# Retention and a channel-mix block on one core: block 0's k tiles made in two steps of six products, and all steps put in a new order

## The chip, the cores and the metric

One core of one Trainium2 chip runs the whole program. The metric is device time in microseconds of one execution. Three runs of the kernel before gave 395.34, 395.37 and 395.74 us, so its median is 395.37 us.

## The reference

`q`, `k`, `v` have 4 batches, 8 heads, 768 tokens and 64 channels, in float32. The first half is retention with a decay per head, `lam`, in steps of 64 tokens; the second is a channel mix over all 512 channels, whose three products are most of the arithmetic.

```python
for b in range(nb):
    intra = np.einsum('bhic,bhjc->bhij', qb, kb) * Dmask[None]
    intra = np.einsum('bhij,bhjd->bhid', intra, vb)
    inter = np.einsum('bhid,bhde->bhie', qb * lam_pow[None], kv_state)
    out[:, :, sl] = intra + inter
    kv_state = lam_block[None, :, None, None] * kv_state + np.einsum('bhsd,bhse->bhde', kb_dec, vb)
...
xk = mu_k * x + (1.0 - mu_k) * x_prev
xr = mu_r * x + (1.0 - mu_r) * x_prev
k = np.maximum(xk @ w_k, 0.0)
v = k * k @ w_v
r = 1.0 / (1.0 + np.exp(-(xr @ w_r)))
return r * v
```

## The kernel before, in words

The tokens are cut into six blocks of 128 (n = 0 to 5), and the heads into four pairs (hp = 0 to 3). Each block goes through retention (scores, decay, values, state), the mix with the token before, and the three products with `w_r`, `w_k` and `w_v`. The weights arrive as 64-bit floats and are put together in the kernel, in block 0's time. For precision each operand of the large products is split in two float32r parts, high and low, and one product is three matmuls of 512 columns (`product`, L420): high by high, high by low, low by high. Only the first half of `w_r` is used unsplit, as float32, in block 0.

The order is written out by hand. `ORDER` (L495) is a string of steps; each step is a letter, a block (or r, k, v for a weight) and an index, and calls one function (table at L464). Every engine keeps the order in which its instructions are issued (`InOrder`, L25), and so does the queue of SyncE, SP, on which all loads are issued. The letters that matter here:

- L, N, H: loads of q, k, v tiles (512 KB, for block 0 also halves). S: load of a weight part (`stage_part`, L176; Sv0 to Sv3 are 1 MB each). c: ScalarE (ACT) copies the part's top bits into `top`. C: VectorE (DVE) puts the word together in place. D: ACT makes the high part (`hir`, `hik`, `hiv`), DVE the low part (`lor`, `lok`, `lov`).
- A scores (`sc`), a their decay (`mw`, `mv`), U state sums (`u`), u and w the next state, B, g and G values (`xp`; g is a one-element copy into `junk` that stands between B and G), q and k decays of queries and keys.
- e, E, f, F: the mix with the token before, for `xk` (small letters) and `xr` (capitals); y, x: its split in `xh` and `xl`.
- R, Q: products with `w_r` for batches 0, 1 and 2, 3 (`r_part`, L402); s: sigmoid into `rt`.
- K: products with `w_k` for one of eight column tiles f (`k_part`, L414), 12 matmuls; h: relu and square into `kf`, in block 0 both on ACT; p: split of two tiles f into `k` (k2).
- V: products with `w_v`, half of the tiles f for one batch (`v_part`, L438); o: multiply with `rt` and store.

PSUM has four buffers of one tag, "m" (`ps_m`, L74), for the tiles rp, kp, vp and from block 1 on xp. A tile that starts must wait until a buffer has been read out: a kp tile by the relu of its h, a vp tile by its o, an rp tile by its s. DMAs on SP use eight semaphores in turn, so a load also waits for the landing of the load eight places earlier.

Of the kernel before, what the change touches and what calls it, by code (L numbers as in the profile page):

```python
# [7 lines left out]
F32 = mybir.dt.float32  # L8
F32R = mybir.dt.float32r
I32 = mybir.dt.int32  # L10
U32 = mybir.dt.uint32
# [7 lines left out]
HP = H // 2  # L19
# [17 lines left out]
def tile_retention_moe(  # L37
# [36 lines left out]
    ps_m = ctx.enter_context(tc.tile_pool(name="ps_m", bufs=4, space=bass.MemoryType.PSUM))  # L74
# [9 lines left out]
    VS, Q, KT, KN = {}, {}, {}, {}  # L84
# [85 lines left out]
    def single(kind, i):  # L170
        return kind + "01"[i % 2] in SINGLE
# [202 lines left out]
    def mix(n, which, hp):  # L374
        t = ts[n, which, hp]
        o = t[:, :, 0:128]
        if n == 0 and which * HP + hp in X32:
            o = X32[which * HP + hp].rearrange("p (b i) -> p b i", b=B)
        vector.scalar_tensor_tensor(o, xp_of(n, hp), mus[:, which, hp:hp + 1], t[:, :, 0:128],
                                    op0=ALU.mult, op1=ALU.add)  # L380

    def split_x(n, which, hp):
        i = which * HP + hp
        if i not in Xhi:
            Xhi[i] = const.tile([128, 512], F32R, tag=f"x{i}", name=f"xh{i}")
        split(Xhi[i].rearrange("p (b i) -> p b i", b=B), Xlo[i].rearrange("p (b i) -> p b i", b=B), ts.pop((n, which, hp))[:, :, 0:128])
# [3 lines left out]
    def product(p, stationary, moving, first, last):  # L390

        passes = PASSES[:2 * len(moving) - 1]
        for i, (s, m) in enumerate(passes):
            tensor.matmul(p, stationary[s], moving[m], start=first and i == 0, stop=last and i == len(passes) - 1)

    def w_of(n, kind, i, c, cols):
        tiles = [W32[kind, i]] if n == 0 and single(kind, i) else [Whi[kind, i], Wlo[kind, i]]
        return [t[:, c, cols] for t in tiles]

    def x_of(n, i, cols=slice(0, 512)):  # L400
        return [t[:, cols] for t in ([X32[i]] if n == 0 and i in X32 else [Xhi[i], Xlo[i]])]

    rps, rt, kps, kfs, k2, vps = {}, {}, {}, {}, {}, {}

    def r_part(n, hp, half):
        for b in (2 * half, 2 * half + 1):
            if hp == 0:
                rps[n, b] = ps_m.tile([128, 512], F32, tag="m", name="rp")
            product(rps[n, b], x_of(n, HP + hp, slice(b * 128, b * 128 + 128)),
                    w_of(n, "r", hp // 2, hp % 2, slice(0, 512)), hp == 0, hp == HP - 1)  # L410

    def r_out(n, b):
        rt[n, b] = work.tile([128, 512], F32, tag="rt", name="rt", bufs=4)
        scalar.activation(rt[n, b], rps.pop((n, b)), AF.Sigmoid)  # L414

    def k_part(n, f):
        kps[n, f] = p = ps_m.tile([128, 512], F32, tag="m", name="kp")
        for hp in range(HP):
            product(p, w_of(n, "k", hp // 2 + f // 4 * 2, hp % 2, slice(f % 4 * 128, f % 4 * 128 + 128)), x_of(n, hp),
                    hp == 0, hp == HP - 1)  # L420

# [38 lines left out]
    def v_out(n, b):  # L460
# [6 lines left out]
        e=lambda n, hp: mix_prev(n, 0, hp), E=lambda n, hp: mix_prev(n, 1, hp),  # L467
        f=lambda n, hp: mix(n, 0, hp), F=lambda n, hp: mix(n, 1, hp),
        y=lambda n, hp: split_x(n, 0, hp), x=lambda n, hp: split_x(n, 1, hp),
        R=lambda n, hp: r_part(n, hp, 0), Q=lambda n, hp: r_part(n, hp, 1), s=r_out, K=k_part, h=k_square, p=k_split, V=v_part, o=v_out,  # L470
        S=stage_part, c=conv_top, C=conv_bits, D=conv_split)
    for step in ORDER.split():
        if step[0] == "Z":
# [19 lines left out]


ORDER = """  # L495
L01 M00 L00 Z10 d01 N01 A01 a01 H01 d02 H00 L02 k01 d00 A00 H02 U01 a00 N00 B01 L03 d03 A02 k00 u01 E01 l00 a02 H03
U00 k02 l02 u00 N02 B00 k03 N03 Sr0 A03 e00 E00 F01 U02 a03 Sr1 Sr2 U03 Sr3 Sk1 u02 u03 cr0 Sk0 e01 B03 E03 cr1 F00
B02 Cr0 f00 L11 Cr1 f01 cr2 L10 E02 R00 Cr2 F03 cr3 Q00 Q01 F02 y00 Dr2 N10 R01 Cr3 x02 e02 Q02 l01 N11 R02 x03 y01
Sk3 Dr3 Q03 N12 R03 f02 ck1 A10 ck0 e03 Ck0 L12 k11 k10 Ck1 f03 y02 Dk0 Dk1 U10 A11 U11 s00 y03 a10 s01 ck3 s02 Sk2
a11 q11 K03 h03 k12 u11 u10 q10 K01 h01 B10 g10 ck2 Sv1 Ck3 Sv0 Ck2 Dk3 A12 G10 s03 Dk2 N13 L13 cv1 K00 Sv3 a12 cv0  # L500
h00 w11 K02 h02 K07 Cv1 K06 l03 E10 Cv0 w10 e10 e11 Sv2 F10 U12 Dv0 E11 f11 f10 k13 p00 F11 p01 h07 A13 U13 q12 q13
K05 K04 cv3 Dv1 cv2 h05 Cv3 L21 a13 V00 Cv2 u13 h06 Dv3 N21 N23 h04 u12 Dv2 V02 B12 g12 A21 p02 y10 p03 G12 V01 x11
o00 x10 L20 e13 V03 y11 V04 e12 q21 N20 E12 o01 F12 f13 f12 a21 V06 V05 Dr0 o02 w12 y12 w13 L23 y13 V07 k20 A20 U20
K10 u20 E13 F13 K11 x12 a20 L22 k21 h10 K16 o03 Q10 x13 Q11 q20 h11 h16 Q12 Q13 U21 B20 A23 u21 N22 g20 A22 G20 p10
s12 k23 s13 N31 K17 h17 E21 K12 N30 q23 F21 e20 e21 a22 h12 p13 K14 f21 L30 k30 w21 K15 w20 E20 f20 h15 a23 h14 K13
k22 h13 F20 R10 x20 U23 L31 U22 B22 R11 u23 R12 g22 y21 u22 p11 q22 R13 G22 w22 o53 w23 A31 y20 A30 k31 q30 U30 E23
U31 s11 e23 e22 N33 s10 V10 a30 x21 E22 F23 L33 f22 F22 y22 f23 a31 V16 V14 p12 V17 u31 x23 V11 o10 V12 V15 x22 y23
u30 V13 o11 o12 N32 K27 o13 K26 Q20 Q21 h27 Q22 h26 Q23 p23 s22 q31 L32 B30 g30 A32 A33 G30 e31 s23 E30 f31 K24 K25
E31 e30 L41 F31 h24 K20 h20 N41 a33 q33 f30 w31 K23 w30 K21 h25 L40 F30 q32 K22 p22 h21 k32 R20 R21 k33 a32 h22 U33
k40 x30 h23 U32 y31 B32 N40 u32 R22 p20 R23 w32 y30 g32 u33 p21 G32 w33 A40 s20 A41 a41 k41 E32 U41 q41 F32 e33 e32  # L510
f33 x32 U40 q40 f32 V20 V21 u40 V22 a40 N43 N42 L42 o20 E33 s21 k42 y33 V23 B40 u41 y32 F33 g40 A42 w41 L43 x31 x33
A43 G40 o21 E41 E40 N50 Q30 e40 Q31 N51 a43 e41 F41 F40 f40 L50 Q32 Q33 s33 q42 K32 f41 V24 V25 s32 k43 K31 h32 V26
a42 K33 V27 h31 h33 K30 w40 L51 h30 K37 o22 k50 p31 R30 R31 q43 R32 R33 x40 o23 U42 h37 s31 U43 u42 u43 B42 g42 A50
A51 G42 s30 L52 q51 K34 K35 p30 h34 K36 a50 h35 E42 y41 y40 e42 a51 L53 h36 F42 e43 V32 V34 f42 f43 q50 x42 w42 p33
V30 p32 V31 y42 x41 y43 V35 o30 V33 E43 N52 o31 N53 V36 k52 V37 F43 K41 K42 o32 k51 w43 U50 x43 o33 u51 B50 g50 u50
A52 h41 A53 G50 h42 E51 a52 K43 e50 F51 h43 e51 K40 a53 E50 f50 K47 p41 F50 f51 K44 K45 h40 p40 h47 K46 h45 h46 R40
q52 R41 h44 k53 p42 R42 R43 B52 U52 u53 g52 s41 q53 s40 Q40 Q41 u52 Q42 Q43 G52 y51 s42 e53 y50 f53 s43 x50 e52 f52
p43 V42 V40 V41 x51 E52 E53 F53 o40 F52 y53 x52 y52 V43 K52 K53 V44 h53 K51 V45 o41 K54 o42 h52 V46 x53 h54 V47 p51
o43 K50 h51 Q50 K55 Q51 h50 h55 Q52 Q53 R50 s53 p50 K57 R51 s52 R52 h57 K56 h56 V52 R53 V50 p52 p53 V51 s50 V56 o50
s51 V53 V54 V55 o51 o52 V57  # L520
"""


# [60 lines left out]
```

## Time and profile before

| what | value |
|---|---|
| median of three runs | 395.37 us |
| the profiled execution: span from first to last instruction | 393.7 us |
| what lies around the span (median less span) | 1.7 us |
| TensorE matmul (PE) busy | 386.9 us, 98% of the span |
| VectorE (DVE) busy | 208.8 us, 53% |
| ScalarE (ACT) busy | 168.5 us, 43% |
| GpSimd (POOL) busy | 23.5 us, 6% |
| granted TensorE clock, mean | 1.000 |

No time of the profiled execution is given besides its span. The busy shares are means over the whole program; the rows further down go by stretch. In a timeline row the first number is the start in us from the span's start, the second how long the row lasts; "xN" merges N instructions, and a bracket says how long the engine had been idle and who ended that. A matmul of 512 columns is shown with some 0.39 us, but the next one starts 0.227 us after it.

### The profile page before, as it was taken

What the parts mean: (1) busy time and instruction counts of PE and PEld (TensorE: products, weight loads), DVE (VectorE), ACT (ScalarE), POOL (GpSimd) and SP (SyncE); (2) the same over time, 40 slices, a digit from 0 to 9 for tenths busy, and PEclk for the clock granted to TensorE, in tenths of its full rate; (3) what the DMA queues carried; (4) which work ended last, traced back from release to release, by engine and by line L of the source; (5) the groups of instructions that cost most, each with busy time, mean ns of one, the idle gap of its engine ahead of it and who ended that gap; (6) DMA issues with size and microseconds to landing.
All of it is one profiled execution on the core that took longest, in us unless ns stands there. A gap on an engine that the chain in (4) does not pass through costs nothing.

```text
span 393.7 us, 9414 instructions
## 1 busy us (share of the span) xinstructions
PE 386.9 (98%) x4154; PEld 317.5 (81%) x4154; DVE 208.8 (53%) x322; ACT 168.5 (43%) x276; POOL 23.5 (6%) x97
## 2 busy tenths in 40 slices
PE   7999999999999999999999999999999999999996
PEld 3757888888888888888888888888888888888885
DVE  4898989763377723358754026573373272232311
ACT  2798999443365412418353023542243360222300
POOL 2121010200001100100110000100000000000000
PEclk9999999999999999999999999999999999999999
DMA  7999861810320502230525001501000000000011
GB/s 265 412 407 412 305 246 55 303 45 28 116 102 11 208 27 82 81 136 2 200 68 219 0 27 42 203 19 64 28 2 1 3 27 27 28 27 0 2 42 65
DMA packets 15560, 42.64 MB, mean 108 GB/s; under 512 B 1440, under 2 KB 1824, under 8 KB 15520
## 3 DMA queue, kind: packets, MB, share of 16 engines
q1 hardware_dynamic: 11920, 35.76, 24.6%
q10 hardware_dynamic: 3600, 6.29, 4.4%
q8 instruction: 32, 0.52, 0.5%
q14 instruction: 8, 0.07, 0.1%
HBM read 35.76 MB, written 6.29 MB: 107 GB/s over the span
## 4 chain that ended last, share of the span: by engine, by line
PE 84%; ACT 8%; DMA 4%; DVE 1%; issue 1%; SPq 1%; POOL 0%; ACTq 0%; POOLq 0%
PE vp L33 32%; PE kp L33 29%; PE rp L33 14%; PE xp L33 4%; DMA wst<-w_r 2%; ACT kf L33 2%; ACT top L33 2%; PE u L33 2%; PE sc L33 2%; DMA in<-first 2%; ACT hiv L33 1%; ACT hik L33 1%; ACT ts L33 1%; SPq L33 1%; ACT xh L33 1%
## 5 line engine op out<-in xcount | busy, mean ns | idle before, releaser
L33 PE MATMUL vp<-hiv,k 128*128 128x512 f32 (+1 forms) x400 | 121.8, 382 | 0.0
L33 PEld LDWEIGHTS vp<-hiv,k 128*128 128x128 f32 x400 | 74.1, 188 | 14.6
L33 PE MATMUL vp<-lov,k 128*128 128x512 f32 (+1 forms) x200 | 76.1, 381 | 0.0
L33 PE MATMUL kp<-xh,hik 128*128 128x512 f32 x192 | 75.6, 394 | 0.3 <-ACT rt L33 0.3
L33 PE MATMUL kp<-xl,hik 128*128 128x512 f32 x192 | 74.8, 390 | 0.0
L33 PE MATMUL kp<-xh,lok 128*128 128x512 f32 x192 | 74.8, 390 | 0.0
L33 ACT ACTIVATE kf<-kp 128x512 f32<-128x512 f32 x48 | 28.3, 595 | 99.3 <-PE kp L33 84.1
L33 DVE TENSOR_TENSOR kf<-kp,kf 128x512 f32<-128x512 f32 x40 | 27.5, 690 | 67.7 <-ACT kf L33 67.6
L33 ACT ACTIVATE ts<-xp,omu 128x512 f32<-128x512 f32 x48 | 31.3, 687 | 29.8 <-DVE rt L33 12.1
L33 PEld LDWEIGHTS vp<-lov,k 128*128 128x128 f32 x200 | 37.6, 188 | 7.1
L33 PEld LDWEIGHTS kp<-xh,hik 128*128 128x128 f32 x192 | 36.0, 188 | 8.5 <-ACT rt L33 0.5
L33 PEld LDWEIGHTS kp<-xh,lok 128*128 128x128 f32 x192 | 36.0, 188 | 7.6
L33 PEld LDWEIGHTS kp<-xl,hik 128*128 128x128 f32 x192 | 36.0, 188 | 7.2
L33 DVE TENSOR_TENSOR xl<-ts,xh 128x512 fp32r<-128x512 f32 x46 | 30.9, 687 | 19.3 <-ACT xh L33 19.3
L33 DVE TENSOR_TENSOR rt<-vp,rt 128x512 f32<-128x512 f32 (+1 forms) x25 | 16.4, 666 | 45.4 <-PE vp L33 43.6
L33 ACT CAST xh<-ts 128x512 fp32r<-128x512 f32 x46 | 27.3, 617 | 25.2 <-DVE rt L33 20.3
L33 DVE SCALAR_TENSOR_TENSOR ts<-xp,mus,ts 128x512 f32<-128x512 f32 x46 | 33.4, 746 | 8.5 <-ACT ts L33 5.5
L33 DVE TENSOR_TENSOR k<-kf,k 128x1024 fp32r<-128x1024 f32 x24 | 29.2, 1222 | 13.0 <-ACT k L33 12.8
L33 PE MATMUL rp<-hir,xh 128*128 128x512 f32 x88 | 35.1, 399 | 0.0
L33 PE MATMUL rp<-hir,xl 128*128 128x512 f32 x88 | 34.3, 390 | 0.0
L33 PE MATMUL rp<-lor,xh 128*128 128x512 f32 x88 | 34.3, 389 | 0.0
L33 ACT CAST k<-kf 128x1024 fp32r<-128x1024 f32 x24 | 24.8, 1048 | 9.4 <-DVE kf L33 7.5
(58 smaller groups left out, 354.3 us busy)
## 6 DMA issues: line engine op xcount, KB each, us to landing
in<-kk SPq DMA_DIRECT2D x20, 512.0 KB, 6.4
in<-qv SPq DMA_DIRECT2D x20, 512.0 KB, 5.5
out<-rt ACTq DMA_DIRECT2D x23, 256.0 KB, 2.0
wst<-w_k SPq DMA_DIRECT2D x4, 1023.8 KB, 12.8
wst<-w_v SPq DMA_DIRECT2D x4, 1023.8 KB, 9.5
in<-first SPq DMA_DIRECT2D x4, 512.0 KB, 5.9
in<-first SPq DMA_DIRECT2D x8, 256.0 KB, 6.6
wst<-w_r SPq DMA_DIRECT2D x4, 511.8 KB, 8.8
```

Of the source, the lines that this page charges most:

```text
L33: return lambda *args, **kw: self.tc.keep_in_program_order(op(*args, **kw))
```

## The change

Two functions are reshaped and the order string is replaced as a whole. `k_part` can now be made in two steps: J (`k_begin`) opens the PSUM tile and makes the six matmuls of head pairs 0 and 1, and the later K makes the six of pairs 2 and 3; where no J came before, K makes all twelve. In the new order each of the eight k tiles of block 0 has a J; the other blocks have none. `r_part` now opens its tile with whichever pair comes first and closes it with the fourth made, so that the order of pairs is free. The work is the same: the same matmuls, casts, loads and stores.

```diff
     def r_part(n, hp, half):
         for b in (2 * half, 2 * half + 1):
-            if hp == 0:
+            first = (n, b) not in rps
+            if first:
                 rps[n, b] = ps_m.tile([128, 512], F32, tag="m", name="rp")
+            done[n, b] = done.get((n, b), 0) + 1
             product(rps[n, b], x_of(n, HP + hp, slice(b * 128, b * 128 + 128)),
-                    w_of(n, "r", hp // 2, hp % 2, slice(0, 512)), hp == 0, hp == HP - 1)
+                    w_of(n, "r", hp // 2, hp % 2, slice(0, 512)), first, done[n, b] == HP)
...
+    def k_begin(n, f):
+        k_pairs(n, f, range(HP // 2))
+
     def k_part(n, f):
-        kps[n, f] = p = ps_m.tile([128, 512], F32, tag="m", name="kp")
-        for hp in range(HP):
+        k_pairs(n, f, range(HP // 2 if (n, f) in kps else 0, HP))
+
+    def k_pairs(n, f, pairs):
+        if (n, f) not in kps:
+            kps[n, f] = ps_m.tile([128, 512], F32, tag="m", name="kp")
+        p = kps[n, f]
+        for hp in pairs:
             product(p, w_of(n, "k", hp // 2 + f // 4 * 2, hp % 2, slice(f % 4 * 128, f % 4 * 128 + 128)), x_of(n, hp),
                     hp == 0, hp == HP - 1)
...
-K05 K04 cv3 Dv1 cv2 h05 Cv3 L21 a13 V00 Cv2 u13 h06 Dv3 N21 N23 h04 u12 Dv2 V02 B12 g12 A21 p02 y10 p03 G12 V01 x11
...
+p00 Sv2 p01 cv2 u12 J07 K07 cv3 h04 h07 u13 Cv2 K06 V00 k21 a13 h05 h06 B12 A21 Cv3 g12 Dv2 p02 p03 G12 Dv3 N22 V02 w13
```

How the new string moves instructions is shown at three places. The first is ACT in block 0, between the split of k2's second tile and the first relus of the second half of k. Before (p01, h07, cv3, Dv1, cv2, h05):

```order
L33 CAST k_1_778<-kf 128x2x512 [waits DVE_49]
L33 ACTIVATE kf<-kp 128x512 [waits DVE_49,PE_49]
L33 ACTIVATE kf<-kf 128x512 [waits Activation_49]
L33 CAST top_101<-wst 128x1024 [waits DMAHW7_49]
L33 CAST hiv_845<-wst 128x1024
L33 CAST top_100<-wst 128x1024 [waits DMAHW0_49]
L33 ACTIVATE kf<-kp 128x512 [waits DVE_49,PE_49]
```

With the change (p01, cv2, cv3, h04, h07):

```order
L33 CAST k_1_826<-kf 128x2x512 [waits DVE_49]
L33 CAST top_100<-wst 128x1024 [waits DMAHW2_49]
L33 CAST top_101<-wst 128x1024 [waits DMAHW1_49]
L33 ACTIVATE kf<-kp 128x512 [waits DVE_49,PE_49]
L33 ACTIVATE kf<-kf 128x512 [waits Activation_49]
L33 ACTIVATE kf<-kp 128x512 [waits DVE_49,PE_49]
```

Both casts of w_v's last parts (the `top` rows, which wait for a DMA) now stand ahead of all four relus of the second half of k, where one relu stood ahead of them; cv2, whose part Sv2 is loaded last, comes first.

The second place is SP's queue of loads in the same stretch, from the first two parts of w_v on. Before (Sv1, Sv0, N13, L13, Sv3, Sv2, L21, N21):

```order
L33 DMA wst<-w_v 128x4095 [waits DMAHW3_49,DVE_49]
L33 DMA wst<-w_v 128x4095 [waits DMAHW4_49]
L33 DMA in<-qv 128x2x512 [waits DMAHW5_49,DVE_49,PE_49]
L33 DMA in<-kk 128x1024 [waits DMAHW6_49]
L33 DMA wst<-w_v 128x4095 [waits DMAHW7_49,DMAHW2_49,DVE_49]
L33 DMA wst<-w_v 128x4095 [waits DMAHW0_49]
L33 DMA in<-kk 128x1024 [waits DMAHW1_49,PE_49]
L33 DMA in<-qv 128x2x512
```

With the change (Sv0, Sv1, L21, N21, L13, N13, Sv3, Sv2):

```order
L33 DMA wst<-w_v 128x4095 [waits DMAHW3_49,DVE_49]
L33 DMA wst<-w_v 128x4095 [waits DMAHW4_49,DVE_49]
L33 DMA in<-kk 128x1024 [waits DMAHW5_49,DVE_49,PE_49]
L33 DMA in<-qv 128x2x512 [waits DMAHW6_49]
L33 DMA in<-kk 128x1024 [waits DMAHW7_49,DVE_49]
L33 DMA in<-qv 128x2x512 [waits DMAHW0_49]
L33 DMA wst<-w_v 128x4095 [waits DMAHW1_49,DVE_49]
L33 DMA wst<-w_v 128x4095 [waits DMAHW2_49]
```

Behind the first load that waits for PE (it is G10, the last reader of block 1's tiles of pairs 0 and 1) stand six loads in both orders; Sv3 and Sv2 were the third and fourth of them and are now the fifth and sixth.

The third place is PE where k begins in block 0, after the state sums U11. Before, K03 with its twelve matmuls:

```order
L33 MATMUL kp<-xh_347,hik_440 128x512 [waits Activation_49]
L33 MATMUL kp<-xl_80,hik_440 128x512
L33 MATMUL kp<-xh_347,lok_441 128x512 [waits DVE_49]
L33 MATMUL kp<-xh_384,hik_440 128x512
L33 MATMUL kp<-xl_81,hik_440 128x512
L33 MATMUL kp<-xh_384,lok_441 128x512
L33 MATMUL kp<-xh_437,hik_444 128x512
L33 MATMUL kp<-xl_82,hik_444 128x512
L33 MATMUL kp<-xh_437,lok_445 128x512 [waits DVE_49]
L33 MATMUL kp<-xh_500,hik_444 128x512 [waits Activation_49]
L33 MATMUL kp<-xl_83,hik_444 128x512 [waits DVE_49]
L33 MATMUL kp<-xh_500,lok_445 128x512
```

With the change, the last of J01's matmuls and the second half of K03 (18 matmuls of J00, J03 and J01, all with `hik_451` and `lok_452`, stand ahead):

```order
L33 MATMUL kp<-xh_327,hik_451 128x512
L33 MATMUL kp<-xl_81,hik_451 128x512
L33 MATMUL kp<-xh_327,lok_452 128x512
L33 MATMUL kp<-xh_428,hik_497 128x512 [waits Activation_49]
L33 MATMUL kp<-xl_82,hik_497 128x512
L33 MATMUL kp<-xh_428,lok_498 128x512 [waits DVE_49]
L33 MATMUL kp<-xh_487,hik_497 128x512
```

The second quarter of w_k (hik_444 before, hik_497 now) was needed seven matmuls after k began and is now needed nineteen after.

## Rows read from the trace of the kernel before

**Rows 1.** Table by stretch: us, then busy us of each engine, clock, DMA share, GB/s.

```profile
18.00:42.00 24.00, 23.60 (x354) 16.68 (x355) 20.91 (x34) 22.03 (x35) 4.11 (x10) 1.00 1.02 410
42.00:67.00 25.00, 24.78 (x276) 20.20 (x278) 22.77 (x30) 24.27 (x34) 1.53 (x7) 1.00 0.56 191
67.00:394.00 327.00, 323.44 (x3340) 269.82 (x3330) 153.01 (x234) 112.61 (x190) 14.92 (x64) 1.00 0.19 68
```

**Rows 2.** Waits of PE over the span: who for whom, us, times, longest.

```profile
PE sc L33 <- DVE mw L33: 1.4, 1, 1.4
...
PE kp L33 <- ACT rt L33: 0.3, 1, 0.3
...
PE xp L33 <- DVE junk L33: 0.2, 1, 0.2
```

**Rows 3.** Timeline of PE and DVE where products with w_r begin.

```profile
20.31 1.68 PE L33 MATMUL rp<-wr,x 128*128 128x512 f32 x3
...
20.07 0.74 DVE L33 SCALAR_TENSOR_TENSOR ts<-xp,mus,ts 128x512 f32<-128x512 f32 x1
```

**Rows 4.** Chain of work that ended last, merged: start, us, what.

```profile
163.58 16.55 PE kp L33 x72
```

**Rows 5.** Timeline of PE: K03's first matmul; then U12, and K05's first behind U13.

```profile
33.27 0.50 PE L33 MATMUL kp<-xh,hik 128*128 128x512 f32 x1 [0.33 <-ACT rt L33]
...
52.64 0.69 PE L33 MATMUL u<-in 64*64 64x64 f32 x32
...
54.20 0.50 PE L33 MATMUL kp<-xh,hik 128*128 128x512 f32 x1
```

**Rows 6.** Timeline of SP (issues): Sk1 with Sk0; N13; Sv3 with Sv2; N21; a later burst's first and last.

```profile
12.81 1.00 SPq L33 DMA_DIRECT2D wst<-w_k  x2
...
41.63 0.55 SPq L33 DMA_DIRECT2D in<-qv  x1
...
45.25 0.80 SPq L33 DMA_DIRECT2D wst<-w_v  x2
...
46.57 18.36 SPq L33 DMA_DIRECT2D in<-qv  x2
...
126.02 0.55 SPq L33 DMA_DIRECT2D in<-qv  x1
...
128.57 0.60 SPq L33 DMA_DIRECT2D in<-kk  x1
```

**Rows 7.** DMA issues, single ones: Sk1; Sv3; N21; the burst's last; us to landing at the end.

```profile
wst<-w_k SPq DMA_DIRECT2D x1, 1023.8 KB, 10.9
...
wst<-w_v SPq DMA_DIRECT2D x1, 1023.8 KB, 6.9
...
in<-qv SPq DMA_DIRECT2D x1, 512.0 KB, 12.1
...
in<-kk SPq DMA_DIRECT2D x1, 512.0 KB, 6.5
```

**Rows 8.** Timeline of ACT: k12's two; h07's relu, cv3, Dv1; h05's relu, h06's relu.

```profile
37.53 0.90 ACT L33 ACTIVATE in<-in,Dt 128x256 f32<-128x256 f32 x2
...
55.18 0.60 ACT L33 ACTIVATE kf<-kp 128x512 f32<-128x512 f32 x1 [0.54 <-DVE k L33]
...
56.35 1.35 ACT L33 CAST top<-wst 128x1024 f16<-128x1024 bf16 x1
57.56 1.04 ACT L33 CAST hiv<-wst 128x1024 fp32r<-128x1024 f32 x1
...
59.74 0.59 ACT L33 ACTIVATE kf<-kp 128x512 f32<-128x512 f32 x1
...
60.90 0.58 ACT L33 ACTIVATE kf<-kp 128x512 f32<-128x512 f32 x1
```

**Rows 9.** Timeline of DVE: Dv2's low part (128x1024), then g12 into junk.

```profile
65.21 1.22 DVE L33 TENSOR_TENSOR lov<-wst,hiv 128x1024 fp32r<-128x1024 f32 x1 [0.47 <-ACT hiv L33]
66.47 0.16 DVE L33 COPY junk<-xp 64x1 f32<-64x1 f32 x1
```

More of the change, by code (lines that the diff above doesn't have):

```diff
@@ L401, in x_of @@
         return [t[:, cols] for t in ([X32[i]] if n == 0 and i in X32 else [Xhi[i], Xlo[i]])]
-    rps, rt, kps, kfs, k2, vps = {}, {}, {}, {}, {}, {}
+    rps, rt, kps, kfs, k2, vps, done = {}, {}, {}, {}, {}, {}, {}
     def r_part(n, hp, half):
         for b in (2 * half, 2 * half + 1):
-            if hp == 0:
+            first = (n, b) not in rps
+            if first:
                 rps[n, b] = ps_m.tile([128, 512], F32, tag="m", name="rp")
+            done[n, b] = done.get((n, b), 0) + 1
             product(rps[n, b], x_of(n, HP + hp, slice(b * 128, b * 128 + 128)),
-                    w_of(n, "r", hp // 2, hp % 2, slice(0, 512)), hp == 0, hp == HP - 1)
+                    w_of(n, "r", hp // 2, hp % 2, slice(0, 512)), first, done[n, b] == HP)
     def r_out(n, b):
@@ L469, in tile_retention_moe @@
         y=lambda n, hp: split_x(n, 0, hp), x=lambda n, hp: split_x(n, 1, hp),
-        R=lambda n, hp: r_part(n, hp, 0), Q=lambda n, hp: r_part(n, hp, 1), s=r_out, K=k_part, h=k_square, p=k_split, V=v_part, o=v_out,
+        R=lambda n, hp: r_part(n, hp, 0), Q=lambda n, hp: r_part(n, hp, 1), s=r_out, J=k_begin, K=k_part, h=k_square, p=k_split, V=v_part, o=v_out,
         S=stage_part, c=conv_top, C=conv_bits, D=conv_split)
@@ L495 @@
 ORDER = """
[L496 to L500, printed above, removed]
@@ L501 @@
-h00 w11 K02 h02 K07 Cv1 K06 l03 E10 Cv0 w10 e10 e11 Sv2 F10 U12 Dv0 E11 f11 f10 k13 p00 F11 p01 h07 A13 U13 q12 q13
-K05 K04 cv3 Dv1 cv2 h05 Cv3 L21 a13 V00 Cv2 u13 h06 Dv3 N21 N23 h04 u12 Dv2 V02 B12 g12 A21 p02 y10 p03 G12 V01 x11
-o00 x10 L20 e13 V03 y11 V04 e12 q21 N20 E12 o01 F12 f13 f12 a21 V06 V05 Dr0 o02 w12 y12 w13 L23 y13 V07 k20 A20 U20
-K10 u20 E13 F13 K11 x12 a20 L22 k21 h10 K16 o03 Q10 x13 Q11 q20 h11 h16 Q12 Q13 U21 B20 A23 u21 N22 g20 A22 G20 p10
-s12 k23 s13 N31 K17 h17 E21 K12 N30 q23 F21 e20 e21 a22 h12 p13 K14 f21 L30 k30 w21 K15 w20 E20 f20 h15 a23 h14 K13
@@ L506 @@
[L506 to L520, printed above, removed]
+L01 Z10 M00 H01 L00 d00 d01 d02 A01 N01 a01 A00 H00 k01 L02 B01 a00 U01 d03 k00 A02 H03 e01 N00 L03 B00 H02 k03 U00 E01
@@ new lines @@
+N03 u01 N02 l01 a02 u00 k02 Sr0 l00 A03 F01 E00 U03 U02 a03 Sr1 u02 F00 u03 B03 cr0 Cr0 Sr3 B02 e00 f00 Q00 Sr2 f01 L11
+E02 cr1 F02 Cr1 y01 R00 Q01 y00 E03 F03 cr2 e02 Cr2 cr3 Cr3 x02 Dr2 x03 Dr3 Sk0 ck0 N10 R01 f02 L10 l02 R02 Q02 N11 k11
+Ck0 k10 Q03 e03 f03 R03 A10 y02 Sk1 s03 A11 Dk0 Sk2 Sk3 L12 s01 ck1 Ck1 U11 a11 s02 y03 J00 Dk1 J03 s00 ck2 u11 J01 ck3
+K03 q11 h03 K01 a10 U10 q10 N12 h01 B10 A12 Ck2 g10 u10 w10 Sv0 Sv1 G10 Dk2 K00 k12 E11 L21 e11 E10 J02 Ck3 N21 a12 l03
+F11 h00 K02 e10 J05 F10 f10 Dk3 w11 cv0 h02 cv1 J04 Cv0 L13 K05 Cv1 Dv0 k13 K04 f11 q12 N13 Dv1 Sv3 J06 A13 U12 U13 q13
@@ new lines @@
+p00 Sv2 p01 cv2 u12 J07 K07 cv3 h04 h07 u13 Cv2 K06 V00 k21 a13 h05 h06 B12 A21 Cv3 g12 Dv2 p02 p03 G12 Dv3 N22 V02 w13
+y11 L22 x10 L20 V01 o00 x11 e13 k20 w12 N20 f13 V03 o01 y10 A20 L23 U21 U20 y13 e12 V06 E13 a20 u20 f12 y12 Dr0 F13 V04
+V05 u21 K12 E12 F12 x12 o02 h12 K10 K13 a21 h13 q20 K11 p11 q21 N23 K16 k22 V07 x13 k23 h16 h10 B20 A22 A23 w20 g20 h11
+G20 K15 e20 E20 o03 f20 L31 F20 e21 f21 E21 L30 a23 F21 p10 K14 h14 h15 K17 Q10 h17 q22 R10 R11 R12 R13 s11 s10 w21 Q11
+a22 N30 p13 q23 y20 Q12 x21 Q13 U22 U23 u23 B22 s12 N31 V10 s13 V12 g22 w23 u22 G22 p12 k31 y21 x20 A31 A30 k30 w22 U31
@@ new lines @@
+e22 E23 e23 f23 y23 f22 q30 V13 V11 o11 u31 V16 o10 L33 V14 V17 y22 o13 F23 E22 L32 V15 o12 K25 F22 h25 k33 N32 x23 K22
+Q20 h22 q31 K23 Q21 x22 h23 Q22 a30 a31 Q23 K24 A32 s22 B30 U30 q32 N33 A33 g30 s23 u30 h24 w31 p22 G30 w30 E30 a33 e30
+N40 L40 e31 E31 K20 f31 h20 K27 p21 k32 N41 F31 h27 K21 f30 U33 F30 U32 a32 B32 h21 R20 R21 R22 u32 o53 R23 u33 w33 L41
+q33 k40 s20 g32 G32 s21 N43 A41 A40 w32 q40 U40 K26 x30 x31 p20 V22 E33 h26 a41 y31 p23 E32 F32 e32 V23 V24 V25 k41 f32
+L42 q41 V20 y32 a40 e33 o21 o22 N42 f33 F33 U41 y30 A42 L43 B40 u40 g40 u41 A43 x33 G40 V21 o20 e41 k42 a43 V26 x32 V27
@@ new lines @@
+y33 K35 E40 o23 K31 L51 h35 E41 h31 w40 K34 f41 q43 K30 F41 h34 Q30 p32 e40 N50 F40 f40 Q31 Q32 h30 k43 Q33 a42 R30 R31
+L50 s32 R32 N51 K33 R33 w41 x41 p30 s33 q42 U43 U42 h33 s30 u42 w42 B42 A51 g42 u43 s31 A50 G42 K32 h32 p31 K36 E42 K37
+h36 y41 V32 L53 h37 y40 L52 e43 w43 f43 V34 p33 F42 x40 e42 V35 N52 f42 y42 V36 E43 V37 k50 F43 y43 o33 a50 V33 a51 V30
+K46 k51 q50 o32 K43 x43 o31 q51 h43 h46 K42 U50 u50 B50 N53 A53 g50 u51 A52 x42 G50 h42 e51 q52 V31 o30 e50 f50 E50 K47
+h47 K41 F50 K44 K45 p41 p43 h44 h45 E51 h41 K40 Q40 Q41 p42 Q42 a53 f51 h40 Q43 s42 R40 F51 y50 q53 k53 s43 R41 p40 y51
@@ L521 @@
+k52 R42 R43 U52 a52 s40 B52 s41 V46 u52 x51 u53 g52 G52 e52 e53 V42 E53 x50 E52 V43 o41 f52 V47 o43 y52 f53 F52 V40 V44
+y53 V41 o40 F53 K51 K53 h51 K52 h53 K50 h50 x52 h52 p50 V45 K55 K56 o42 p51 h55 Q50 K57 h57 Q51 Q52 x53 Q53 K54 s52 h56
+h54 V54 p52 p53 R50 R51 s53 V55 R52 R53 V52 s51 s50 o52 V56 V53 o51 V50 V51 o50 V57
 """
```

## The prediction

> **What bounds the kernel now.** The table by stretch is read first [rows 1]. From 67 us on PE is busy 323.4 of 327 us while DVE has 153 and ACT 113: there PE alone sets the pace, and the rest of its 3.6 us is the run-out behind the last matmul. The clock is granted at 1.00 in every stretch. So the tail of 327 us is a fixed sum of matmuls, and the change leaves that sum as it is: no matmul is added or removed, and the runs of large products are broken by small ones sixteen times in both orders. What can move is the first 67 us, where DVE and ACT are full (20.9 and 22.0 of 24 us, then 22.8 and 24.3 of 25) and the DMA engines run at 410 GB/s until 42 us. The list of PE's waits is read second [rows 2]: the 1.4 us of the second scores behind the first decay (one `sc` buffer) stay in the new order, and what is left is a kp behind rt (0.3) and an xp behind junk (0.2), with some tenths where the first products begin. That is all that a better order can win, about 1 us of 395; the DMA queue and ACT between 42 and 60 us are where a worse one can lose.
>
> A measurement of this kernel can tell about 0.2%, 0.8 us, from no change.
>
> **What is won.** Three terms.
>
> - First products with w_r: the seventh and eighth of sixteen float32 records wait for a PSUM buffer that f01 reads out. Its row ends at 20.81; three records there take 1.68 us, where 16 are 0.43 apart otherwise [rows 3]. f01 stood behind Cr1, which waits for a load; it now stands ahead of it. Won 0.2 us. The start of these products hangs on the same landing of Sr0 with the same number of bytes ahead, a cast and a DVE step: nothing.
> - K03 waits for s00's buffer, idle 0.33 us, and with the 0.1 us of restarting 0.4 us [rows 2, 5]. With the J steps s03, s01 and s02 free buffers one after another and J00 needs only the first quarter of w_k. Won 0.4 us, if the second quarter is there for the second half of K03. It is near: Sk1 landed at 12.8 + 10.9 = 23.7 us [rows 6, 7]; in the new queue L11, Sk0, N10, L10 and N11, 3.15 MB, stand ahead of it, 7.7 us at 410 GB/s [rows 1], so 31.4. Its cast 1.36, C 1.2, high part 1.05 and low part 1.2 us [rows 8, 9] with 0.2 us of handing over end at 36.4. On PE J00 starts at 33.27 less 0.6 us won, less 0.5 us for U10, which now stands behind K01: 32.15. Eighteen matmuls at 0.23 [rows 4] end at 36.3, and the low part is read by the third after that, at 36.8. It fits by 0.4 us.
> - G12 waits 0.22 us, with its restart 0.3 us, for g12, which stands on DVE behind a low part of 1.22 us [rows 2, 9]. In the new order Cv3 is ahead of g12 and the low part behind it. Won 0.3 us.
>
> Sum 0.9 us. Cost of the J steps themselves: a tile of twelve matmuls cut in two has the same loads and matmuls; 0. The rest of the reordering (loads of later blocks, q, k and w steps, order of tiles f) lies under PE's work from 67 us on, where DVE and ACT are half idle; 0, and if that cover were gone each late step would cost its own 0.6 to 1.2 us.
>
> **What is lost.** The new order puts all four PSUM buffers in one hand: K05, K04, J06/K06 and J07/K07 fill them, and V00 gets its buffer from h04's relu. Ahead of h04 on ACT now stand cv2 and cv3, and cv2 waits for Sv2, now the sixth load behind G10 where it was the fourth. So the question is when Sv2 lands, counted from the end of G10.
>
> What is queued there: ACT does not pass a waiting instruction. At 55.18 it had idled 0.54 us for h07 while cv3 behind it, whose part Sv3, issued at 45.25, had landed 6.9 us later, at 52.2, began only at 56.35 [rows 6 to 8]. The Trainium skill, TensorE: Matmul & The Clock Gate, in its note on engine queue depths, says that ScalarE and VectorE are strict first-in-first-out; the trace agrees. Were it otherwise, h04 would go ahead and only the 0.9 us won would be left.
>
> PE's way from G10 to V00: 66 large matmuls, at 16.55/72 us each [rows 4] 15.2, and A13, U12 and U13 with 54.20 - 52.64 = 1.55 us [rows 5] and 0.15 us of changing over: 16.9 us. From Sv2's landing to V00: two casts, 57.56 - 56.35 = 1.21 each, 2.4, a relu 0.6 [rows 8], handing over 0.1: 3.1 us. So V00 waits when Sv2 lands later than 13.8 us after G10.
>
> That landing the trace does not show; bounds from both sides. All six loads are 4.2 MB. Low end: their bytes at 410 GB/s from the first moment on, 10.2 us [rows 1]. High end: the same six sizes in the old order, from N13's issue at 41.63 to N21's landing at 46.57 + 12.1 = 58.67, 17.0 [rows 6, 7]. Between: a burst of four 512 KB loads from an idle queue, 126.02 to 128.57 + 6.5 = 135.07, 9.05 us, and behind it, with the queue deep again, 2.1 MB at the full stretch's 410 GB/s, 5.1 us [rows 1, 6, 7]: 14.15. I take that: the burst is the nearest row to the first four loads, and Sv3 and Sv2 are issued some 4 us ahead of their turn, as the loads of the full stretch were. V00 then waits 0.35 us.
>
> Behind it: B12 needs h05's relu. Between h04's and h05's relus lie a square, h07's pair and k21: 0.6 + 1.16 + 0.8 + 0.6 = 3.1 us [rows 8] against 2.8 us of V00, so 0.3 us more, and the last low part of w_v then comes about as late behind V01: 0.3 us. Both are hidden when V00 does not wait. Lost 1.0 us.
>
> **Sum.** 393.7 - 0.9 + 1.0 = 393.8 us of span; with 1.7 us around it, by which the median of the runs exceeds it, 395.5 us.
>
> **Rivals.**
>
> 1. The six loads run at the full rate, Sv2 lands by 13.8 us, and nothing waits. For it: the stretch of 24 us at 410 GB/s held loads of the same kinds and sizes. Against it: 191 GB/s from 42 us on, where the queue had run dry, and 9.05 us for half as many bytes at 126 us. Time: 395.4 - 0.9 = 394.5 us. The Trainium skill names a figure too: DMA: Bandwidth & Descriptors, in Anatomy of one DMA, fits 2.0 us and bytes at 436 GB/s (for DMAs issued by GpSimd), which makes 11.6 us for 4.2 MB, an estimate; by that rule this rival holds, while the trace's six loads took 17.0.
> 2. Slower: the loads take as long as they did. It is the same place, V00 behind h04 behind cv2; price one us for each us that Sv2 lands after 13.8, with 0.6 us behind it. From 14.1 us on it outweighs the 0.9 us won; at 17.0, less half a us for Sv3's late issue in the old order, V00 waits 2.7: 395.4 - 0.9 + 3.3 = 397.8 us. For it: the same six loads measured. Against: in the old order Sv3 was held back by Dk2 until 45.25, and the queue was shallow.
> 3. The J steps win nothing, since the second quarter of w_k is later than 36.8: 1:1 from there. 0.4 us of reserve over a chain of five steps. With 1 us late and the forecast's wait: 396.2 us or more, though a late G10 also moves the loads.
>
> **How the numbers follow.** Forecast (landing between 13.8 and 14.9): 0.42, time 395.5, its own range 394.7 to 396.1. Rival 1: 0.24. Rival 2: 0.26. Rival 3: 0.08. Range: 394.4 (everything won) to 397.7; beyond lies the end of rival 2. Faster by over 0.2% (under 394.6) needs rival 1 with all three terms: 0.22. Within 0.2%: the forecast, a little of rival 1 and half of rival 3: 0.47. Slower: rival 2 and the rest of 3: 0.31.
>
> **What would show it.** Right: PE's waits have no kp behind rt and no xp behind junk; an ACT wait of `top` for the DMA of w_v between 53 and 60 us; PE's vp waits for ACT kf, 0.1 to 1 us, and then xp. The six loads take 13 to 15 us from first issue to last landing. Wrong: no wait of PE behind G12 at all (rival 1), one of over 1.5 us at vp (rival 2), a wait of kp for lok near 36 us (rival 3), or any PE wait of more than 0.3 us after 70 us, for which I see no cause.

## The result and the profile after

| | before | changed |
|---|---|---|
| median, us (6 runs each) | 395.71 | 398.06 |
| lowest and highest, us | 395.34, 397.32 | 397.38, 399.43 |
| profiled execution: span, us | 393.7 | 397.7 |
| first product with w_r, last matmul, us | 18.06, 390.17 | 19.41, 394.12 |

The ratio is 1.0063, 95% interval 1.0050 to 1.0077: slower, by about 2.4 us (2.0 to 3.0 by the interval), where 395.5 us and a range of 394.4 to 397.7 were forecast. The profiled execution of the changed kernel was the longest of its six runs (its span and 1.7 us are 399.4), so single waits below are this execution's, and what they are worth as a rule is told by the runs further on.

The table by stretch of the changed kernel (us, then busy us of each engine, clock, DMA share, GB/s) answers to [rows 1]:

```profile
18.00:42.00 24.00, 23.06 (x272) 16.20 (x269) 20.80 (x33) 22.76 (x36) 2.99 (x10) 1.00 1.02 410
42.00:67.00 25.00, 23.68 (x414) 19.50 (x410) 20.54 (x28) 22.32 (x33) 1.73 (x7) 1.00 0.48 179
67.00:394.00 327.00, 325.62 (x3301) 271.37 (x3291) 155.87 (x235) 116.17 (x192) 15.14 (x64) 1.00 0.19 68
```

PE is busy 1.1 us less between 42 and 67 us and ACT 2 us less: both waited there. The list of PE's waits answers to [rows 2]:

```profile
PE sc L33 <- DMA in<-first: 2.6, 1, 2.6
PE vp L33 <- ACT kf L33: 1.3, 1, 1.3
PE idle L33 <- DVE zeros L33: 1.2, 1, 1.2
PE sc L33 <- DMA in<-qv: 1.0, 1, 1.0
PE rp L33 <- DVE wr L33: 0.9, 1, 0.9
PE vp L33 <- DVE lov L33: 0.3, 1, 0.3
```

The kp behind rt and the xp behind junk are gone, as forecast. New are the vp behind kf (V00, forecast), a vp behind lov (V01), an sc behind a load (A20, not forecast), and a longer start: the second scores A00 wait for a load (they waited for the first decay), and the first product for Cr0.

The timeline of ACT (start, us, work, idle before it) shows the first of them from ACT's side:

```profile
54.44 1.98 ACT L33 CAST k<-kf 128x1024 fp32r<-128x1024 f32 x2
58.84 2.58 ACT L33 CAST top<-wst 128x1024 f16<-128x1024 bf16 x2 [2.41 <-DMA wst<-w_v]
61.28 0.59 ACT L33 ACTIVATE kf<-kp 128x512 f32<-128x512 f32 x1
```

Behind p00 and p01, ACT idles 2.41 us; then come cv2 and cv3, then h04's relu, which ends at 61.87. In PE's timeline V00's first matmul starts 0.05 us later; V01's low part and A20 follow:

```profile
61.92 0.50 PE L33 MATMUL vp<-hiv,k 128*128 128x512 f32 x1 [1.32 <-ACT kf L33]
...
72.50 0.50 PE L33 MATMUL vp<-lov,k 128*128 128x512 f32 x1 [0.34 <-DVE lov L33]
...
77.69 0.69 PE L33 MATMUL sc<-in 64*64 64x64 f32 x32 [1.04 <-DMA in<-qv]
```

The list of waits leaves out what PE needs to get going again. By starts of matmuls (the step from the matmul before, less the step that is usual there) these three cost 1.5, 0.5 and 1.1 us.

The loads that stand behind these waits, in SP's timeline (L21, which G10's end releases; Sv3 with Sv2; the first and last of the four loads that G12's end releases: N22 and N20):

```profile
43.72 0.33 SPq L33 DMA_DIRECT2D in<-kk  x1
...
45.98 1.50 SPq L33 DMA_DIRECT2D wst<-w_v  x2
...
67.70 0.55 SPq L33 DMA_DIRECT2D in<-qv  x1
...
69.98 0.55 SPq L33 DMA_DIRECT2D in<-qv  x1
```

and Sv2, then N20, among the DMA issues (the last number is us to landing):

```profile
wst<-w_v SPq DMA_DIRECT2D x1, 1023.8 KB, 12.0
...
in<-qv SPq DMA_DIRECT2D x1, 512.0 KB, 7.6
```

Sv2 was issued at 46.83 and landed at 58.8, 15.1 us after G10's end. N20 landed at 77.6, 9.9 us after G12's end and 0.1 us ahead of A20.

### The profile page after: what moved, and what is told of

Read it like the earlier page. It is cut to its first block, busy times and chain, and to the rows that moved or that the text cites. A ratio compares the mean times of both kernels' runs of the same rounds, so it can differ in the third digit from the quotient of the medians.

```text
span 397.7 us, 9430 instructions
## 1 busy us (share of the span) xinstructions
PE 386.7 (97%) x4154; PEld 317.8 (80%) x4154; DVE 208.9 (53%) x322; ACT 169.5 (43%) x276; POOL 23.0 (6%) x97
## 4 chain that ended last, share of the span: by engine, by line
PE 86%; DMA 9%; ACT 2%; SPq 1%; issue 1%; DVE 1%; DVEq 0%
PE vp L33 31%; PE kp L33 29%; PE rp L33 17%; PE xp L33 4%; DMA wst<-w_v 3%; PE sc L33 2%; PE u L33 2%; DMA wst<-w_r 2%; DMA in<-qv 2%; DMA in<-first 2%; SPq L33 1%; ACT kf L33 1%; ACT top L33 1%; ACT ts L33 0%; ACT hiv L33 0%
## 5 line engine op out<-in xcount | busy, mean ns | idle before, releaser
L33 DVE TENSOR_TENSOR rt<-vp,rt 128x512 f32<-128x512 f32 (+1 forms) x25 | 16.7, 666 | 49.2 <-PE vp L33 49.2
```

Of the source, the lines that this page charges most:

```text
L33: return lambda *args, **kw: self.tc.keep_in_program_order(op(*args, **kw))
```

## The experiments

The first four runs had their runs of the kernel before in common (median 395.54), and so had each later group (395.61, 395.56, 395.74, 395.91). Ratios are to these. Each trace below is one execution.

### The two places of loads

**L20 and N20 first (e1)**

```diff
-N22 V02 w13 y11 L22 x10 L20 V01 o00 x11 e13 k20 w12 N20
+L20 N20 N22 V02 w13 y11 L22 x10 V01 o00 x11 e13 k20 w12
```

> The two loads for A20 (L20, N20) are issued ahead of N22 and L22, which A22 reads two tiles of v later. Theory: A20's 1.1 us wait at 77.7 us is N20 landing as the last of a burst of four 512 KB loads that all start at G12's end; as the second of the burst it lands some 5 us after G12, when 8.9 us of PE's work lie between: the wait goes, the waits at V00 (1.5 us) and V01 (0.5 us) stay; 1.1 us less, about 397.0 us, 1.003 of the kernel before. Rival, that A20 is late for another reason (a scores buffer, or the whole queue being behind): unchanged, 398.1 us.

397.87 us, ratio 1.0055 (1.0043 to 1.0067). The sc behind in<-qv is gone from PE's waits, and from the first product to the last matmul the trace has 373.52 us against 374.71. The time does not show it: 397.0 us were expected, the median is 0.2 us below the changed kernel's, and the two intervals overlap.

**Sv3 and Sv2 ahead of L21 and N21 (e2), and both moves (e3)**

```diff
-G10 Dk2 K00 k12 E11 L21 e11 E10 J02 Ck3 N21 a12
+G10 Dk2 K00 k12 E11 e11 E10 J02 Ck3 a12
...
-p00 Sv2 p01 cv2
+p00 Sv2 L21 N21 p01 cv2
```

> L21 and N21 are issued behind Sv3 and Sv2, not ahead of them, so that Sv2 is the fourth of the six loads and not the sixth. Theory: Sv2 lands some 2.5 to 3 us earlier, 12 to 12.5 us after the end of G10; ACT's 2.4 us wait for it goes, h04's relu is in time, and V00 (1.5 us) and V01 (0.5 us) do not wait; A20's load starts at G12's end as before, so A20 then waits the 0.5 us that V01 no longer takes, 1.6 us in all: 1.5 us less, about 396.6 us. Rival, that V00 waits because ACT is full of other work ahead of h04: V00's wait stays within 0.3 us of 1.5 and the time at 398.

> Both moves of loads together. Theory: no PE wait over 0.3 us behind G10; 3.1 us less than the changed kernel, about 395.0 us, 0.998 of the kernel before, as only the 0.9 us won ahead of 67 us is left, less what the start may cost. Rival, that the first products start later in the new order by itself (1.35 us in the profiled run): 395.0 only if that is chance, else about 396.0.

e2: 396.60 us, 1.0021 (1.0010 to 1.0032). Sv2 lands 12.6 us after G10's end (43.71 to 56.34), V00 and V01 wait no more, and PE has one wait behind its first product, for N20:

```profile
PE sc L33 <- DMA in<-qv: 0.8, 1, 0.8
PE rp L33 <- DVE wr L33: 0.3, 1, 0.3
```

e3: 395.44 us, 0.9996 (0.9987 to 1.0004). No wait is left behind the first product. Medians fall by 1.5 us from the changed kernel to e2 and by 1.2 us more to e3; by the other way, over e1, they fall by 0.2 and then by 2.4 us. So the two places together are the whole loss, within what can be told (e3 a second time, s3 below, had 1.0008), but how it divides between them depends on which is put right first. And e3 is level with the kernel before, though it takes 371.16 us from the first product to the last matmul where that took 372.10. Its first product started late, at 20.02.

**h04 ahead of cv2 (e4)**

```diff
-p01 cv2 u12 J07 K07 cv3 h04 h07
+p01 h04 cv2 u12 J07 K07 cv3 h07
```

> Loads as in the changed kernel; h04 stands ahead of cv2 on ACT. Theory: cv2 still idles for Sv2 until it lands 15 us after G10, but h04's relu is done before, and V00's wait of 1.5 us goes; cv3, h07 and all behind come 1.25 us earlier, so V01 waits 0.7 us for the last low part of w_v and A20 0.9 us for N20: 1.5 us less, about 396.6 us. Rival, that V00 needs something else of Sv2 than ACT's place in the line: V00's wait stays.

397.84 us, 1.0058 (1.0046 to 1.0071): my number was wrong. V00's wait is gone, so it was ACT's line; but the same lateness now meets PE one step on, at B12, whose buffer h05's relu frees behind the same cv3:

```profile
PE xp L33 <- ACT kf L33: 1.1, 1, 1.1
PE vp L33 <- DVE lov L33: 0.4, 1, 0.4
```

ACT's timeline has h04's relu well ahead of the place where it stood at 61.28, and behind it cv2 and cv3:

```profile
57.55 0.60 ACT L33 ACTIVATE kf<-kp 128x512 f32<-128x512 f32 x1 [2.07 <-DVE k L33]
58.18 0.63 ACT L33 ACTIVATE kf<-kf 128x512 f32<-128x512 f32 x1
58.71 2.57 ACT L33 CAST top<-wst 128x1024 f16<-128x1024 bf16 x2
```

### The J steps

**Without them (e7)**, on e3's order:

```diff
-J00 Dk1 J03 s00 ck2 u11 J01 ck3
+Dk1 s00 ck2 u11 ck3
...
```

> The kernel with both moves of loads, without the J steps: each tile of k is made whole where its K step stands. Theory: K03 now starts where J00 did and reads the second quarter of w_k after six matmuls; its high part is ready about 3 us behind that start and its low part 4.2 us behind: PE waits 2.5 to 3 us in two pieces, 398.2 us. Rival, that the J steps only hide the 0.4 us that the old order lost there: 395.8 us.

398.89 us, 1.0080 (1.0058 to 1.0103), some 3.3 us above e3's order, 2.6 us of it between the first product and the last matmul in the two traces. PE waits for Dk1 in two pieces:

```profile
35.96 0.50 PE L33 MATMUL kp<-xh,hik 128*128 128x512 f32 x1 [1.20 <-ACT hik L33]
...
37.22 0.50 PE L33 MATMUL kp<-xh,lok 128*128 128x512 f32 x1 [0.53 <-DVE lok L33]
```

By starts these are 1.4 and 0.7 us, and a third is 0.2. So the J steps do their work in this order: they pay for Dk1's later place, which the old order did not have.

### Where the gain behind the first product goes

**L00 second (e5)**, and the opposite in the kernel before (e6)

```diff
-L01 Z10 M00 H01 L00 d00
+L01 Z10 M00 L00 H01 d00
```

```diff
-L01 M00 L00 Z10 d01 N01 A01 a01 H01 d02
+L01 M00 Z10 d01 N01 A01 a01 H01 L00 d02
```

> The kernel with both moves of loads, and L00 issued ahead of H01 at the start, as in the kernel before. Theory: the new order's first products start late (19.4 us where the kernel before has 18.1) since the second scores A00 wait for L00, which lands 0.9 to 1.8 us later behind H01; PE is in order and has no reserve until the first products, so every tenth counts. With L00 second, A00 waits for its decayed weights alone, PE idles no more than 1.6 us there, and only the gain of the new order is left: 394.8 to 395.1 us, 0.998 to 0.999 of the kernel before. Rival, that the late start is chance of the first transfers and of the clock and has nothing to do with the order: 395.4 us, as with both moves.

> The kernel before with L00 issued behind H01 (and N01, which stays ahead of it). Theory: A00 waits for L00, which now lands about 8.3 us, and PE's chain to the first products moves with it: 0.4 to 1.0 us more, about 396.2 us. Rival, that the place of L00 costs nothing: 395.5 us.

395.51 us, 0.9996 (0.9982 to 1.0011), and 396.07 us, 1.0004 (0.9993 to 1.0015). In e5 A00 waits for the decay again, but the first product still started at 18.78, now behind Cr0. Neither time differs from the kernel before by what can be told, and in e6 A00 still waited for the decay: that one load's place is the cause is not shown.

**The whole opening exchanged.** The 56 steps ahead of the first product, in the old order ahead of e3's rest (r9), in the new order ahead of the old rest (r10), the loads of it alone in the old order (r11), and in the old order ahead of the changed kernel's rest (s4). The first rows of r9:

```diff
-L01 Z10 M00 H01 L00 d00 d01 d02 A01 N01 a01 A00 H00 k01 L02 B01 a00 U01 ...
+L01 M00 L00 Z10 d01 N01 A01 a01 H01 d02 H00 L02 k01 d00 A00 H02 U01 a00 ...
```

> The kernel with both moves of loads; its 56 steps ahead of the first product stand in the order of the kernel before, on all engines, and everything from the first product on as in the new order. In six traces with the new opening the first product started at 18.5 to 20.0 us, in three with the old one at 18.1 to 18.6. Theory: the opening's order costs about 0.8 us, and it is this that eats the 0.95 us won behind it; first product at 18.0 to 18.6, 394.7 us, 0.998 of the kernel before. Rival, that the gain behind the first product is only a late start being made up (ACT and DVE are full, and what PE finds ready does not come sooner): the first product is earlier, but waits appear on PE between it and 45 us, and the time stays at 395.4 to 395.6 us.

> The kernel before with those 56 steps ahead of its first product in the new order. Theory: first product at 18.5 to 20 us, 0.8 us slower, 396.4 us. Rival, that the later start is made up behind it by waits that go (the seventh record of the first products, K03's): 395.6 to 395.9 us.

> The kernel with both moves of loads; of the 56 steps of the opening only the loads stand in the old order (L00 and N01 ahead of H01, H02 and H03 exchanged, N02 ahead of N03). If the late start comes from the transfers' order: like the whole old opening, 394.7 us. If from the order of the work on PE, ACT and DVE (u03 behind u00 on one buffer, 0.3 us): 395.4 us.

> The changed kernel with its 56 steps ahead of the first product in the order of the kernel before, and nothing else undone. Theory: the opening's order is worth 0.8 to 1.4 us, so 396.8 us here, with the waits at V00, V01 and A20 as they were. Rival, that the old opening gains nothing in front of the new order (the kernel with both moves gained nothing from it): 398.0 us.

r10: 396.97 us, 1.0029 (1.0018 to 1.0041): the new opening costs the kernel before 1.1 us (0.7 to 1.6). In its trace, of its shortest run (396.24 us), the first product comes at 18.53 and K03 at 34.12, 0.85 us later than in [rows 5], still with a wait for rt; so some 0.5 us of this lie ahead of the first product and 0.4 behind it. r11: 396.43, 1.0015 (1.0003 to 1.0027): slower too, and in its trace PE's u waits 1.4 us for st. r9: 395.42, 0.9994 (0.9980 to 1.0008), no gain over e3. s4: 397.98, 1.0048 (1.0033 to 1.0063), no clear gain over the changed kernel either; V00 waits 1.7 us there, with Sv2 15.6 us behind G10's end, and A20 waits 0.1 us. So the exchange of openings costs 1.1 us ahead of the old rest and nothing that can be told ahead of the new one.

**Second traces**: the kernel before unchanged (r12), r9 again (s1), e3 again (s3).

> The kernel before, unchanged, for a second trace of its start. If its first product starts again at 18.0 to 18.6 us with K03's wait behind it, the comparison of starts holds; if it comes at 19 us in this execution, the start scatters by itself as much as between the two orders.

> The kernel with both moves of loads and the old opening once more, for a trace of an execution near its median: the trace of its first run was one of its three longest (first product at 20.07 us). Theory, that PE is then bound by what ACT and DVE make: first product at 18.0 to 18.5 us and 0.3 to 0.8 us of waits on PE between it and 45 us (x parts of the third step, or Dk0's low part at J00). Rival, that the order is free of waits: no such wait, and a time of 394.7 us.

> The kernel with both moves of loads once more, for a trace near its median: the first was its slowest run, with the first product at 20.02 us because N02 landed 1.5 us late. Theory: first product at 18.6 to 19.0 us, 371.2 us from there to the last matmul, no wait between, 395.3 us. Rival, that its gain was only a late start made up: first product at 18.1 us and 0.5 us or more of waits behind it.

r12 is the kernel before in a run of 397.09 us (median of the eight 395.63), first product and K03's first matmul:

```profile
20.20 1.13 PE L33 MATMUL rp<-wr,x 128*128 128x512 f32 x2 [1.73 <-DVE wr L33]
...
34.96 0.50 PE L33 MATMUL kp<-xh,hik 128*128 128x512 f32 x1
```

It started 2.1 us later than in its first trace: 14.76 us lie between the two, not 15.21, and 371.60 us to the last matmul. The seventh record does not wait, and K03 starts 0.34 us behind the matmul before it, not 0.55 (in e3 it is 0.15), so of K03's 0.4 us some 0.2 are left. So half of the 0.94 us that e3 shows behind its first product is what the kernel before shows too when it starts late. s1, in a run of 395.36 us (median 395.39; 0.9992, 0.9973 to 1.0010), first product and J00's first matmul:

```profile
18.60 2.84 PE L33 MATMUL rp<-wr,x 128*128 128x512 f32 x6 [0.32 <-DVE wr L33]
...
33.00 0.50 PE L33 MATMUL kp<-xh,hik 128*128 128x512 f32 x1
```

14.40 us, 371.46 us to the last matmul, and by starts one wait of 0.2 us at 26 us: 0.6 us less than the first trace of the kernel before. Two traces of one kernel can differ as much (e8 and s2 below: 371.37 and 372.10), so this is no gain that is shown. s3 had a median of 396.62 us, 1.0008 (0.9992 to 1.0024), with the first product at 19.86 behind a stretch at half clock (see below).

**f01 and s00 in the kernel before (e8, and s2 again)**

```diff
-f00 L11 Cr1 f01 cr2
+f00 L11 f01 Cr1 cr2
...
-Dk0 Dk1 U10 A11 U11 s00
+Dk0 s00 Dk1 U10 A11 U11
```

> The kernel before with two steps moved and no J step: f01 ahead of Cr1 on DVE, and s00 ahead of Dk1 on ACT. Theory: the first products no longer wait in the middle (0.2 us), and K03's buffer comes free 0.5 us sooner (0.4 us): 394.9 us, 0.9985 of the kernel before. Rival, that K03 then waits as long for Dk1's parts, which only J steps cure: 395.3 us.

> The kernel before with f01 ahead of Cr1 and s00 ahead of Dk1 once more, for a second trace: the first had its first product at 18.58 us, 14.57 us ahead of K03, and no wait between. Theory, that the start scatters and the gain is there behind it: again 14.6 us from first product to K03. Rival, that a first product at 18.1 us meets ACT's and DVE's parts too early: 14.9 to 15.1 us, with waits.

395.74 us, 1.0002 (0.9989 to 1.0016), and 395.60 us, 0.9985 (0.9969 to 1.0001): no gain that can be told. The first trace had 14.57 us from first product (18.58) to K03 and no wait; the second 15.30 us (18.52), with Sr1 landing at 19.61 and 0.3 us of wait by starts inside the products. K03's own wait is gone in both, without a J step. The rival holds in part: the later parts of w_r can set this stretch too.

**PE filled ahead of A00 (t1 on e3, t2 on r9)**

```diff
-a01 A00 H00
+a01 Z3 A00 H00
```

> The kernel with both moves of loads and the new opening, with three empty matmuls (0.6 to 1.3 us) between A01 and A00, where PE idles 1.6 to 2.9 us. Theory: where PE idles over 2 us there, with L00 third in the queue, the granted clock falls to half until about 12 us in some executions (13 of 63 runs with the new opening had a mean clock of 0.996 or less), and costs 1 to 1.5 us; filled, the clock stays at full and the first product starts at 18.5 to 19.0 us: 395.2 us, no run with a clock under 0.997. Rival, that the clock falls for reasons that PE's idling there does not set: as many slow clocks as before, 395.5 to 396.6 us.

> The same three empty matmuls in the kernel with both moves of loads and the old opening, which had a first product at 18.60 us and 0.2 us of wait behind it in a run of 395.36 us. Theory: PE idles only 1.6 us at A00 there and the clock seldom falls; the fill gives nothing, 395.4 us. If the fill also makes the clock rise sooner, A01 ends sooner: 394.9 us, which would be the first version clearly below the kernel before.

395.76 us, 0.9993 (0.9980 to 1.0005), and 395.73 us, 0.9997 (0.9984 to 1.0009). None of these 24 runs had a mean clock of 0.996 or less, where 13 of 63 with the new opening had and 3 of the 23 of the kernel before beside these two. At 13 of 63, twelve runs of t1 without one would come by chance once in 16 times, so that the fill keeps the clock up is likely and not shown. Neither median moved beyond its interval. In t1's trace the first product came at 19.20, with a wait of 1.0 us for Cr0 ahead of it, whose load Sr0 landed at 17.63: with the clock at full, that landing sets it. In t2's trace V01 waits 0.4 us for its low part again, so V01 is without a wait in most traces with both moves, not in all.

## Why the prediction was wrong, by its steps

**What is won.** The three terms are there as waits that went (the seventh record's, K03's, G12's): 372.10 us from first product to last matmul become 371.2 to 371.4 in both traces of e3, 0.7 to 0.9 us against 0.9. Rival 3 did not come: Sk1 landed at 31.9 us (forecast 31.4), and no kp waits in the changed kernel. What failed is to count them against one execution: when its first product is late, the kernel before itself loses the seventh record's wait and half of K03's (r12), so the gain against it is then some 0.4 us.

The sentence that the start gives "nothing" failed too. It went by bytes ahead of Sr0, which are the same, and did not follow PE's own chain. From A00 to the first product PE took 9.65 us before and 10.07 in r10, where u and xp wait 0.3 and 0.2 us; in e4, where A00 starts at 8.86 and not at 8.46, the new opening takes 9.60. Nor did the 1.4 us of A00 simply stay: with L00 third in the queue A00 waited 1.6 to 2.6 us for that load in five of eight traces (with the old opening 1.4 to 1.7 us). r10 prices the exchange at 1.1 us ahead of the old rest. Won and start come to about nothing together: e3 is at 0.9996. How much each of them is worth in the new order is not shown, as r9, with the old opening, is at 0.9994.

**What is lost at V00.** The chain held link by link. V00 would have been ready 16.7 us after G10's end (forecast 16.9); from Sv2's landing to V00's first matmul passed 3.1 us (forecast 3.1); so the threshold of 13.8 us was right to some tenths. The term that was mis-sized is the landing: 15.1 us after G10's end, forecast 14.15. That makes 1.3 us, and 1.5 were measured against 0.35. Behind it B12 did not wait and V01 waited 0.5 (forecast 0.3 each): 2.0 us in place of 1.0. By the medians, putting Sv2 right wins 1.5 us alone (e2), since A20 then takes over some of it, and 2.4 us where A20's load is right already (e1 to e3). It is rival 2, at 15.1 and not at its end of 17.0.

Why 14.15 was short: it joined a burst for the first half, 9.05 us, with 410 GB/s for the second, 5.1 us. The fourth of the six loads landed 9.2 us behind G10's end, as the burst had it; Sv3 and Sv2, the last two in the queue, took 5.9 us more. So the second half failed: the rate of a stretch with many loads queued was taken for the end of a queue. All six, 4.2 MB in 15.1 us, went at 278 GB/s; in the four traces with this order of loads Sv2 landed 14.5 (e4), 15.1 (e1), 15.1 (changed) and 15.6 us (s4) behind G10's end.

The estimate from the Trainium skill (DMA: Bandwidth & Descriptors, Anatomy of one DMA), 11.6 us for these bytes as one transfer, is further off. The rule of the Trainium skill's note on engine queue depths (TensorE: Matmul & The Clock Gate), that ScalarE's queue is strictly first in, first out, agrees with the rows: behind the waiting cv2 h04's relu started at 61.28, 17.6 us behind G10's end, and ahead of it, in e4, at 57.55, 14.8 us behind G10's end there.

**The step that failed outright** is "the rest of the reordering ... lies under PE's work from 67 us on ... 0". A20 was moved from behind V07 to behind V03, and its load N20 is the last of four that start only at G12's end. The prediction had the price in its rows: such a burst takes 9.05 us [rows 6, 7]. PE has V02, V01 and V03 in between, 8.4 us in this trace without their wait. That DVE and ACT are half idle there says nothing of a load that cannot start sooner. It cost 1.1 us in the profiled execution, where the burst took 9.9 us, and 1.2 us from e2 to e3. In s4 and e4, where Sv2 is late too, it cost 0.1 us and none: the burst took 8.8 and 8.5 us there, and V01's wait of 0.5 us gives it 8.9 us of cover. That fits e1, which wins 0.2 us: while V01 waits, a quick burst is mostly hidden, and without V01's wait A20 pays. The prediction had named the sign itself: a wait of more than 0.3 us after 70 us, for which it saw no cause.

**The sum.** Measured 2.4 us slower, forecast 0.1. By the runs the two places of loads together are 2.6 us (changed to e3), of which the forecast had 1.0, and of the 0.9 us won nothing that can be told is left. The range ended at 397.7, the high end of one rival alone; none held a second place of lost time.

**What stays open.** The first product came at 18.06, 18.15, 18.52, 18.58 and 20.20 us in the five traces of the kernel before and its variants with the old opening (e6, e8, s2, r12), at 18.60, 18.79, 18.85 and 20.07 with the old opening ahead of the new rest (s1, s4, t2, r9), and at 18.46 to 20.02 in ten with the new one, seven of them at 19.0 or later. So the new opening tends to start later, but the start scatters by 2 us in one and the same kernel. Only ahead of the old rest is a cost in time shown (r10); why it is not seen ahead of the new rest (r9, s4) stays open, and so does the split between PE's gaps, the landing of Sr0 and the clock. No version clearly beats the kernel before.

## What to carry to other kernels

When an order of steps is changed, list for every step that moves earlier the loads it reads, with the event that lets each be issued, and put the landing of its place in the burst against PE's work in between; an idle ACT or DVE does not cover a load. Do not price loads behind a dry queue by the rate of a full one, not even the last of them (14.15 us against 15.1 here), and keep the scatter of a landing (14.5 to 15.6 us) in the range. A wait is won only against the same start: where the engines ahead are full, a later start can make part of it vanish by itself.

## What the runs showed of the hardware

PE's granted clock can fall in the opening. In s3's trace (columns as in [rows 1]) A00 had waited 2.2 us for L00, and from 9 to 11 us the clock was 0.50, the lower of its two levels (1.2 GHz):

```profile
7.00:9.00 2.00, 0.25 (x2) 0.28 (x4) 0.91 (x2) 0.91 (x2) 0.00 (x0) 0.90 1.04 388
9.00:11.00 2.00, 2.00 (x18) 1.77 (x19) 0.14 (x1) 0.91 (x2) 0.00 (x0) 0.50 1.04 414
11.00:13.00 2.00, 2.00 (x34) 1.93 (x34) 2.00 (x6) 0.44 (x1) 0.00 (x0) 0.74 1.04 409
```

PE did 18 matmuls from 9 to 11 us, in the changed kernel's profile 44. The clock fell at the same place in the traces of e1 and e2, behind waits of 1.9 and 2.1 us. In the changed kernel's profile PE had waited 2.6 us there and kept its clock, so the length of the wait alone does not decide it.

The same four loads behind G12 took 8.5 us (e4), 8.8 (s4), 8.9 (e2) and 9.9 (changed) from first issue to N20's landing: A20's margin is smaller than this scatter, and e4 shows no wait there.
